# Batch 0 of clustered attention with a token mixer: mixed tokens turned by VectorE in 32x32 blocks, stored and gathered by DMAs, in place of transposes on TensorE

## The chip, the cores and the metric

One core of a Trainium2 chip runs the kernel. The metric is the device time of one execution in microseconds (us), lower is better. The runs of one kernel agree to within about 0.2%.

## The reference

Everything is in float32. Attention over B = 4 batches, H = 8 heads, S = 768 tokens, D = 64, where a query sees only the keys of its own cluster of 16; its output x then goes through a mixer over the tokens and one over the channels:

```python
q_assign = argmax(q_n . c_n)             # cosine, 16 centroids for each head
k_assign = argmax(k_n . c_n)
scores = where(q_assign == k_assign, q @ k.T / 8, -1e9)
x = softmax(scores) @ v                  # heads side by side: (4, 768, 512)
u = x + ((x.T @ U) @ V).T                # U 768x32, V 32x768: tokens mixed
out = u + relu(u @ w_ch1) @ w_ch2        # 512 -> 2048 -> 512
```

## The kernel before

**Attention** goes by 16 pairs of heads, four for each batch (`NP = 4`); a pair's heads i lie in 128 partitions. For each pair the tokens are assigned to clusters (`sims`, `clusters`), the row maxima are found from products on TensorE that VectorE reduces (`rowmax`: matmuls in line 2174, reductions in 2176), the scores are made transposed and go through the exponential on ScalarE (`scores`, 2202 and 2204), the sums are collected on GpSimd and VectorE (`weights`, 2232), the products with V are made (`values`, 2240), and the result is turned back and divided by the sums into `xt`, tokens in partitions (`normalise`, 2273 and 2274). The products of `rowmax`, `clusters`, `mix_v` and others share four PSUM banks (pool `ps_w`, `work(name)`).

**The mixer over tokens** follows at the end of each batch. `mix_u` and `mix_sum` make x^T U. For batch 0 `mix_v` (matmul in 2324, addition on VectorE in 2325) adds the product with V to `xt` itself, so that `xt` holds u; `store_u` writes it to the DRAM tensor `u_scr`. For batches 1 to 3 `turn_x` (2285) turns each pair's part of `xt` in blocks of 32x32 on VectorE, in halves h of 384 tokens, and `store_x` (2290) writes that to the DRAM tensor `x_blk`; later `fetch_columns` (2542) gathers it from there with the channels in partitions, in pieces of 128 bytes.

**The channel mixer** needs u with channels in partitions, in a high and a low part of FP32R type. For batch 0 it runs as a plain product, in two halves i of 384 tokens: `fetch_u` loads 384x512 of u from `u_scr` into the buffer "R" (2357); `turn_u(i, d)` makes, for each of four blocks d of 128 channels, three transposes on TensorE into a PSUM bank (2363), a copy on ScalarE to the high part (2365) and a subtraction on VectorE to the low part (2366); `gemm1` (2374 to 2376), `after_gemm1` (2383), `gemm2` (2393 to 2395) and `finish` follow for 16 blocks of the hidden width. `finish` adds the rows that `fetch_u` loaded. Batches 1 to 3 run by seven products of half-sized blocks (`seven1`, `seven2`).

**The order** is written out by hand. The planner collects events `at(time, function, arguments)`; the times come from the tables `times`, `mixes` and `stages`, and the table `shifts` moves single events. They are sorted by time, each function issues its instructions, and `keep_order` (line 1827) keeps every engine in just that order. The unit of time is one step of the attention's loop; `M0` is the start of batch 0's `gemm1`. SyncE (SP) issues the DMAs, in the same order. The lines that set the events of the steps here:

```python
if i >= NP:
    at(when(f"normalise{h}", i) + 0.35, turn_x, i, h)
    at(when(f"normalise{h}", i) + 0.9, store_x, i, h)
...
at(m + (-11.79 if i else -15.06), fetch_u, i)
for d in range(ND):
    at(m + (-4.5 + d if i else -7 + 0.6 * d), turn_u, i, d)
```

Which of a pool's buffers a tile gets is left to the pool, by turns.

The engines in the views: PE is TensorE's matmuls, PEld its weight loads, DVE VectorE, ACT ScalarE, POOL GpSimd. "Busy" of PE counts pipelined records, which overlap.

## Time and profile before

| what | value |
|---|---|
| time, median of 3 runs | 909.28 us |
| lowest and highest of the runs | 909.24 and 911.18 us |
| profiled execution, first to last instruction | 908.0 us |
| PE busy in the whole span | 893.4 us |
| DVE, ACT, POOL busy in the whole span | 734.8, 451.0, 614.7 us |
| granted TensorE clock, mean | 1.000 |

The profile shows one execution. Its span is the time from its first to its last instruction; the device time of the runs also counts what lies around that, 1.28 us by the median. A time of its own is not given for the profiled execution, so the span stands beside the runs' median. A busy engine is not yet the one that sets the time: the chain that ended last tells on whom the end waits, and the list of waits of an engine when it stood still and for whom.

### The profile page before, as it was taken

Reading aid. Unit: us, or ns where it says so; the run is one execution under the profiler, and the core shown is the slowest. Engines: PE = TensorE matmul, PEld = TensorE weight load, DVE = VectorE, ACT = ScalarE, POOL = GpSimd, SP = SyncE. Lnnn points to the kernel's source line nnn. Section 1 sums busy time; section 2 is a strip of 40 time slices with the busy share of each in tenths; the row PEclk is TensorE's granted clock in tenths of the full one; section 3 lists DMA queues with packets and bytes.
Section 4 is the critical chain, followed back from the end, with each engine's and each line's share of the span. In section 5 each row is a group of like instructions: output and inputs, shape, how many; then the busy total and the mean of one; then the engine's idle time right before and its main releaser. Section 6 shows DMA issues by size and latency. Waiting matters only on the chain.

```text
span 908.0 us, 15012 instructions
## 1 busy us (share of the span) xinstructions
PE 893.4 (98%) x5157; PEld 762.2 (84%) x5157; DVE 734.8 (81%) x1387; ACT 451.0 (50%) x801; POOL 614.7 (68%) x472
## 2 busy tenths in 40 slices
PE   5999999999999999999999999999999999999998
PEld 2767767777677777768898999999999999999998
DVE  7999989999999997798885366767889778897777
ACT  6646555555555556674755444533334424363330
POOL 3678759998879999962748856733578424875337
PEclk9999999999999999999999999999999999999999
DMA  8765845777486763678998996998676997769653
GB/s 228 182 155 139 205 119 145 225 196 183 127 203 162 200 174 83 184 240 265 287 305 283 294 366 240 322 308 276 222 286 214 354 248 295 258 241 327 233 194 116
DMA packets 123068, 206.25 MB, mean 227 GB/s; under 512 B 46545, under 2 KB 90385, under 8 KB 118513
## 3 DMA queue, kind: packets, MB, share of 16 engines
q1 hardware_dynamic: 122464, 205.10, 73.4%
q8 instruction: 41, 0.67, 0.3%
q10 hardware_dynamic: 528, 0.20, 0.1%
q14 instruction: 35, 0.28, 0.1%
HBM read 131.96 MB, written 42.83 MB: 193 GB/s over the span
## 4 chain that ended last, share of the span: by engine, by line
PE 95%; ACT 2%; DMA 1%; DVE 0%; SPq 0%; POOL 0%; issue 0%; ACTq 0%; DVEq 0%
PE st L2202 14%; PE o_ps L2240 14%; PE ps_max L2174 7%; PE ps_q L2684 4%; PE ps_q L2686 4%; PE ps_q L2685 4%; PE ps_p L2609 4%; PE ps_p L2608 4%; PE ps_p L2610 4%; PE ps_p L2686 3%; PE ps_p L2684 3%; PE ps_p L2685 3%; PE ps_q L2608 3%; PE ps_q L2609 3%; PE ps_q L2610 3%; PE ps_h L2374 3%
## 5 line engine op out<-in xcount | busy, mean ns | idle before, releaser
L2176 DVE TENSOR_REDUCE m<-ps_max 128x1 f32<-128x384 f32 x384 | 189.8, 548 | 17.4 <-PE ps_max L2174 15.0
L2232 POOL TENSOR_TENSOR T<-T,pr 128x768 f32<-128x768 f32 x95 | 178.7, 1885 | 21.9 <-DVE T L2232 13.3
L2204 ACT ACTIVATE pr<-st 128x768 f32<-128x768 f32 x192 | 154.6, 812 | 69.0 <-PE st L2202 58.1
L2202 PE MATMUL st<-arena 128*128 128x384 f32 (+1 forms) x768 | 169.4, 344 | 0.0
L2202 PEld LDWEIGHTS st<-arena 128*128 128x128 f32 (+1 forms) x768 | 137.3, 190 | 4.3 <-issue 1.8
L2240 PE MATMUL o_ps<-pr,vt 128*64 128x384 f32 x768 | 129.8, 490 | 0.0
L2240 PEld LDWEIGHTS o_ps<-pr,vt 128*64 128x64 f32 x768 | 52.8, 137 | 66.8 <-issue 62.4
L2174 PE MATMUL ps_max<-arena 128*128 128x384 f32 x384 | 106.3, 358 | 2.2 <-DVE arena L2139 1.5
L2174 PEld LDWEIGHTS ps_max<-arena 128*128 128x128 f32 x384 | 70.8, 194 | 14.6 <-DVE m L2176 4.9
L2608 PE MATMUL ps_p<-arena,w 128*128 128x384 f32 x186 | 62.2, 334 | 0.0
L2610 PE MATMUL ps_p<-arena,w 128*128 128x384 f32 x186 | 62.2, 334 | 0.0
L2609 PE MATMUL ps_p<-arena,w 128*128 128x384 f32 x186 | 62.2, 334 | 0.0
L2232 POOL TENSOR_TENSOR T<-pr 128x768 f32<-128x768 f32 x23 | 43.6, 1896 | 18.9 <-ACT pr L2204 18.8
L2608 PE MATMUL ps_q<-arena,w 128*128 128x384 f32 x150 | 50.2, 334 | 0.0
L2610 PE MATMUL ps_q<-arena,w 128*128 128x384 f32 x150 | 50.2, 334 | 0.0
L2609 PE MATMUL ps_q<-arena,w 128*128 128x384 f32 x150 | 50.1, 334 | 0.0
L2244 ACT COPY os<-o_ps 128x384 f32<-128x384 f32 x32 | 15.2, 480 | 65.3 <-PE o_ps L2240 62.0
L2101 POOL TENSOR_TENSOR arena<-R,arena 128x768 fp32r<-128x768 f32 x17 | 31.8, 1870 | 22.2 <-ACT arena L2096 22.1
L2232 POOL TENSOR_TENSOR Tv<-Tv,pr 128x768 f32<-128x768 f32 x21 | 40.3, 1921 | 4.1 <-DVE Tv L2232 3.0
L2670 POOL TENSOR_TENSOR h<-ring,h 128x384 fp32r<-128x384 f32 x17 | 17.6, 1032 | 37.6 <-ACT h L2660 18.6
L2609 PEld LDWEIGHTS ps_p<-arena,w 128*128 128x128 f32 x186 | 34.9, 188 | 0.1
L2608 PEld LDWEIGHTS ps_p<-arena,w 128*128 128x128 f32 x186 | 34.9, 188 | 0.1
(588 smaller groups left out, 2354.1 us busy)
## 6 DMA issues: line engine op xcount, KB each, us to landing
w<-wc SPq DMA_DIRECT2D x24, 1024.0 KB
w<-wc SPq DMA_DIRECT2D x25, 768.0 KB
arena<-wc SPq DMA_DIRECT2D x19, 768.0 KB
rw<-in_w SPq DMA_DIRECT2D x27, 512.0 KB
R<-in_qk SPq DMA_DIRECT2D x32, 384.0 KB
arena<-arena SPq DMA_DIRECT2D x31, 384.0 KB
arena<-arena SPq DMA_DIRECT2D x62, 192.0 KB
wc<-f SPq DMA_DIRECT2D x46, 256.0 KB
```

What stands on the lines that cost most here:

```text
L2174: nc.tensor.matmul(ps[:, 0:HS], x1[:, 0, g // 2, g % 2, t * P:(t + 1) * P], x1[:, 1, h, g % 2, :], start=True, stop=True)
L2176: nc.vector.reduce_max(live["m2", i][:, h, u:u + 1], ps[:, 0:HS], axis=AX.X)
L2202: nc.tensor.matmul(st[:, k, 0:HS], keys, x[0:rows_, 0, h, j, :], start=not last, stop=last)
L2204: nc.scalar.activation(pr, st[:, :, 0:HS], AF.Exp, scale=SCALE)
L2232: eng.tensor_add(T, live["p", i, h, 0] if c == 1 else T, live["p", i, h, c])
L2240: nc.tensor.matmul(o_ps[64 * j:64 * j + 64, 0:HS], vv[:, c, j, :], chunk(i, h, c, j), start=(c == 0), stop=(c == NT - 1))
L2608: nc.tensor.matmul(ps, w[:, 0, k], u[:, 0, k], start=(k == 0), stop=False)
L2609: nc.tensor.matmul(ps, w[:, 0, k], u[:, 1, k], start=False, stop=False)
L2610: nc.tensor.matmul(ps, w[:, 1, k], u[:, 0, k], start=False, stop=(k == 1))
L2684: nc.tensor.matmul(ps, w[:, 0], h[:, 0], start=(j == 0), stop=False)
L2685: nc.tensor.matmul(ps, w[:, 0], h[:, 1], start=False, stop=False)
L2686: nc.tensor.matmul(ps, w[:, 1], h[:, 0], start=False, stop=(j == 1))
```

## The change

- `x_blk[0]` becomes a DRAM tensor as for the other batches. Batch 0's four pairs go through `turn_x` and `store_x` too, behind `mix_v`, so that what is stored is u in blocks of 32x32: eight block transposes on VectorE and eight stores.
- A new `fetch_turned(h, d)` gathers these, four DMAs for each h and d (32 in all), each 32 partitions of 12 pieces of 32 elements, into a buffer `uT` of tag "R", channels in partitions.
- `turn_u` no longer uses TensorE or PSUM: the copy to the high part and the subtraction read `uT`.
- `fetch_u` moves to M0 and M0 + 9; the second half's `turn_u` moves ahead.
- A table `slots` with a class `Placed` hands out the buffers of several pools in a written order.
- Some 500 events of the plan move, by changed and added entries of `shifts`.

```diff
-    x_blk = [None, *(dram.tile([NT, P, DM], F32, name=f"x_blk{b}") for b in range(1, B))]
+    x_blk = [dram.tile([NT, P, DM], F32, name=f"x_blk{b}") for b in range(B)]
...
-    def turn_u(i, d):
-
-        ps = work("ps_uT")
-        for t in range(HT):
-            nc.tensor.transpose(ps[:, t * P:(t + 1) * P], live["u", i][:, t, d * P:(d + 1) * P], ident)
-        hi, lo = (x[:, d, :] for x in turned[i % 2])
-        nc.scalar.copy(hi, ps[:, 0:HS])
-        nc.vector.tensor_sub(lo, ps[:, 0:HS], hi)
+    def fetch_turned(h, d):
+
+        if ("uT", h) not in live:
+            live["uT", h] = rows.tile([P, ND, HS], F32, name="uT", tag="R")
+        x = x_blk[0].rearrange("(h t) (a r) (d k c) -> h d k r (t a) c", h=2, a=4, d=ND, k=4)[h, d]
+        y = live["uT", h][:, d].rearrange("p (n c) -> p n c", c=32)
+        for k in range(4):
+            nc.sync.dma_start(out=y[32 * k:32 * k + 32], in_=x[k])
+
+    def turn_u(h, d):
+
+        x = live["uT", h][:, d]
+        hi, lo = (x[:, d, :] for x in turned[h])
+        nc.scalar.copy(hi, x)
+        nc.vector.tensor_sub(lo, x, hi)
...
             if i >= NP:
                 at(when(f"normalise{h}", i) + 0.35, turn_x, i, h)
                 at(when(f"normalise{h}", i) + 0.9, store_x, i, h)
+            else:
+                at(NS * NP + (17.0, 13.0)[1 - h] + (1.6, 1.8)[1 - h] * i, turn_x, i, h)
+                at(NS * NP + (17.01, 13.01)[1 - h] + (1.6, 1.8)[1 - h] * i, store_x, i, h)
...
-        at(m + (-11.79 if i else -15.06), fetch_u, i)
         for d in range(ND):
-            at(m + (-4.5 + d if i else -7 + 0.6 * d), turn_u, i, d)
+            at(M0 + (-19.9 if i else -29.9) + 2 * d, fetch_turned, i, d)
+        at(M0 + (9 if i else 0), fetch_u, i)
+        for d in range(ND):
+            at(m + (-14.5 + 1.2 * d if i else -7 + 0.6 * d), turn_u, i, d)
...
+class Placed:
...
+    def tile(self, shape, dtype, name, tag=None, **kind):
+        turn = self.turns.get(tag or name)
+        if turn is not None:
+            return self.pool.tile(shape, dtype, name=name, tag=f"{tag or name}_{next(turn)}", bufs=1)
+        if tag is not None:
+            kind["tag"] = tag
+        return self.pool.tile(shape, dtype, name=name, **kind)
```

Where the rows of the instructions move, by the line numbers of each program (a line from 2050 on stands some 247 lines later in the changed one):

TensorE, in batch 3 of attention, shortly ahead of the expert layers of batch 0. Before, three and six transposes of u stand between the scores (`st`) and the products with V (`o_ps`):

```order
L2202 MATMUL st<-arena 128x384 x8
L2186 MATMUL ps_mT<-ident,m 12x128
L2363 MATMUL ps_uT<-ident,u 128x128 x3
L2240 MATMUL o_ps<-pr,vt 64x384 x10
L2260 MATMUL ps_sumT<-ident,sums 128x128 x3
L2273 MATMUL ps_oT<-ident,os 128x128 x3
L2202 MATMUL st<-arena 128x384 x8
L2363 MATMUL ps_uT<-ident,u 128x128 x6
L2202 MATMUL st<-arena 128x384 x8
L2240 MATMUL o_ps<-pr,vt 64x384 x14
```

The same place in the changed program:

```order
L2433 MATMUL ps_mT<-ident,m 12x128
L2499 MATMUL ps_sum<-T,sel 32x384 x2
L2499 MATMUL ps_sum<-Tv,sel 32x384 x2
L2487 MATMUL o_ps<-pr,vt 64x384 x10
L2507 MATMUL ps_sumT<-ident,sums 128x128 x3
L2520 MATMUL ps_oT<-ident,os 128x128 x3
L2449 MATMUL st<-arena 128x384 x8
L2487 MATMUL o_ps<-pr,vt 64x384 x14
L2449 MATMUL st<-arena 128x384 x8
```

The transposes are gone, the sums of a pair (`ps_sum`) come earlier, and the products with V stand ahead of the next scores.

VectorE, in batch 1 of attention, where the additions of `mix_v` (`xt<-ps_h,xt`) stand among the reductions of the row maxima (`m<-ps_max`). Before:

```order
L2325 TENSOR_TENSOR xt<-ps_h,xt 128x512
L2176 TENSOR_REDUCE m_1634<-ps_max 128x1 x4
L2325 TENSOR_TENSOR xt<-ps_h,xt 128x512
L2176 TENSOR_REDUCE m_1634<-ps_max 128x1 x2
L2325 TENSOR_TENSOR xt<-ps_h,xt 128x512
L2176 TENSOR_REDUCE m_1634<-ps_max 128x1 x8
L2176 TENSOR_REDUCE m_1937<-ps_max 128x1
```

The changed program from the same addition on:

```order
L2572 TENSOR_TENSOR xt<-ps_h,xt 128x512
L2423 TENSOR_REDUCE m_1635<-ps_max 128x1 x2
L2532 STREAM_TRANSPOSE xs_1844<-xt 128x384
L2423 TENSOR_REDUCE m_1635<-ps_max 128x1 x3
L2572 TENSOR_TENSOR xt<-ps_h,xt 128x512 x2
L2423 TENSOR_REDUCE m_1635<-ps_max 128x1 x5
L2532 STREAM_TRANSPOSE xs_1924<-xt 128x384
L2572 TENSOR_TENSOR xt<-ps_h,xt 128x512
L2423 TENSOR_REDUCE m_1635<-ps_max 128x1
L2532 STREAM_TRANSPOSE xs_1941<-xt 128x384
```

The first three block transposes (`xs`) stand there now, between the reductions; the other five follow with one to five reductions or some work of the clusters between them.

SyncE, some way ahead of the expert layers. Before:

```order
L2318 DMA x_scr_93<-x_2993 96x512
L1875 DMA rw<-in_w 128x512
L2056 DMA vt<-in_v 128x768
L1875 DMA rw<-in_w 128x512
L2357 DMA u<-u_scr 128x1536
```

And in the changed program, where the gathers (`uT`) stand:

```order
L2197 DMA arena<-ones 1x12x128 x2
L2613 DMA uT<-x_blk_90 32x12x32 x4
L2122 DMA rw<-in_w 128x512 x2
L2673 DMA wc_0_99<-w_98 256x1x256 x2
L2613 DMA uT<-x_blk_90 32x12x32 x4
L2537 DMA x_blk_92<-xs_4406 128x3x128
L2613 DMA uT<-x_blk_90 32x12x32 x12
```

The load of u is gone from here (it is issued later); 20 of the 32 gathers stand among loads of weights (`rw`).

## Rows read from the trace of the kernel before

**Rows 1.** The page: span, and the chain that ended last by engine.

```profile
span 908.0 us, 15012 instructions
...
PE 95%; ACT 2%; DMA 1%; DVE 0%; SPq 0%; POOL 0%; issue 0%; ACTq 0%; DVEq 0%
```

**Rows 2.** PE's waits, the longest: waiting line, releaser, us in total, times, longest.

```profile
PE ps_c L1994 <- ACT rw_g L1992: 7.5, 2, 5.1
```

**Rows 3.** Stretch, its us; busy us of PE, PEld, DVE, ACT, POOL; clock, DMA, GB/s.

```profile
65.00:900.00 835.00, 835.00 (x4876) 724.03 (x4877) 673.49 (x1255) 412.80 (x731) 576.81 (x410) 1.00 0.74 231
150.00:195.00 45.00, 45.00 (x280) 33.90 (x278) 41.36 (x81) 27.55 (x39) 42.38 (x25) 1.00 0.66 199
336.00:390.00 54.00, 54.00 (x344) 39.15 (x342) 42.09 (x84) 32.32 (x51) 52.24 (x30) 1.00 0.52 141
440.00:480.00 40.00, 40.00 (x211) 36.48 (x210) 32.64 (x53) 25.45 (x50) 19.72 (x16) 1.00 0.88 282
```

**Rows 4.** Tile of the transposes: duration in ns min/median/max, first and last start.

```profile
L2363 PE MATMUL ps_uT<-ident,u x24: 270/272/328, 380.5 to 471.4; 128*128 128x128 f32 x24
...
L2366 DVE TENSOR_TENSOR arena<-ps_uT,arena x4: 519/532/551, 383.8 to 404.9; 128x384 fp32r<-128x384 f32 x4
```

**Rows 5.** PE's timeline in the expert layers: start, us, instruction.

```profile
466.46 0.39 PE L2395 MATMUL y<-arena,hx 128*128 128x512 f32 x1
466.69 0.49 PE L2363 MATMUL ps_uT<-ident,u 128*128 128x128 f32 x3
466.93 0.42 PE L2374 MATMUL ps_h<-arena,w1h 128*128 128x384 f32 x1
467.19 0.34 PE L2375 MATMUL ps_h<-arena,w1h 128*128 128x384 f32 x1
467.36 0.34 PE L2376 MATMUL ps_h<-arena,w1l 128*128 128x384 f32 x1
```

**Rows 6.** PE's timeline in attention, each group of transposes with what follows.

```profile
380.48 0.49 PE L2363 MATMUL ps_uT<-ident,u 128*128 128x128 f32 x3
380.90 3.45 PE L2240 MATMUL o_ps<-pr,vt 128*64 128x384 f32 x20
...
386.40 0.82 PE L2363 MATMUL ps_uT<-ident,u 128*128 128x128 f32 x6
386.97 1.67 PE L2202 MATMUL st<-arena 128*128 128x384 f32 x8
...
401.38 0.55 PE L2363 MATMUL ps_uT<-ident,u 128*128 128x128 f32 x3
401.68 0.59 PE L2202 MATMUL st<-arena 128*128 128x384 f32 x2
```

**Rows 7.** DVE: the block transposes by line, and the page's group of row maxima.

```profile
L2285 DVE STREAM_TRANSPOSE xs<-xt x24: 520/569/579, 190.0 to 447.1; 128x384 f32<-128x384 f32 x24
...
L2176 DVE TENSOR_REDUCE m<-ps_max 128x1 f32<-128x384 f32 x384 | 189.8, 548 | 17.4 <-PE ps_max L2174 15.0
```

**Rows 8.** Gathers of batches 1 to 3: SP's issue, and DMA of 500 to 524 us.

```profile
L2542 SPq DMA_DIRECT2D f<-x_blk x48: 309/525/3347, 500.3 to 744.1; - x48
...
DMA packets 17212, 6.79 MB, mean 283 GB/s; under 512 B 12158, under 2 KB 17111, under 8 KB 17209
...
f<-x_blk SPq DMA_DIRECT2D x16, 96.0 KB
```

**Rows 9.** Timelines of DVE and POOL: an operation with two inputs in SBUF.

```profile
388.94 1.82 DVE L1924 TENSOR_TENSOR arena<-rw_t,arena 128x512 fp32r<-128x512 f32 x1
393.20 0.68 DVE L1924 TENSOR_TENSOR arena<-rw_t,arena 128x512 fp32r<-128x512 f32 x1
...
384.54 7.91 POOL L2232 TENSOR_TENSOR T<-T,pr 128x768 f32<-128x768 f32 x4
```

**Rows 10.** DVE's timeline at the first expert block; the matmuls that need it.

```profile
414.93 1.02 DVE L2383 SCALAR_TENSOR_TENSOR hx<-ps_h,hx 128x384 fp32r<-128x384 f32 x2
...
L2393 PE MATMUL y<-w,hx x24: 387/390/500, 419.3 to 500.1; 128*128 128x512 f32 x24
```

748 lines of the change are left out of this document (490 added, 258 removed).

## The prediction

> **What bounds the kernel now.** I read the page's chain that ended last first: 95% of it is TensorE (PE), everything else is 2% or less [rows 1]. Then PE's own list of waits: the longest entry is 7.5 us, for the centroids at the program's start [rows 2]; what follows it in the list is smaller still. Then the busy time by stretches: from 65 to 900 us PE is busy in 835.00 of 835.00 us, at a granted clock of 1.00 [rows 3], which is the upper of its two levels (2.4 GHz). So in the whole part that the change touches PE never stands still, and two things follow: a microsecond of PE work that is taken out shortens the run by a microsecond, and any other engine costs something only from the moment when PE waits for it. VectorE (DVE), GpSimd (POOL) and the DMA engines are all less than full over that stretch [rows 3], so the question for each is local: is it late in one place.
>
> **The sum, step by step.** It is made against the profile's span of 908.0 us [rows 1]. The median of the three runs, 909.28, stands 1.28 us above that span, for what lies around it, and I add the same 1.28 at the end.
>
> *1. PE loses 24 transposes.* The trace records 272 ns for each [rows 4], which would be 24 x 0.272 = 6.5 us. But PE works pipelined, and its records overlap, so I go by starts. They stand in eight groups of three, and each group can be priced by when the work behind it starts. In the expert stage, a matmul that stands in front of another starts 0.23 us before the next thing, the group of three takes 0.24 us from its start to the next start, and the first matmul behind it takes 0.26 us to the second, where matmuls without a neighbour of another kind are 0.17 us apart [rows 5]. So a group costs 0.24 + 0.09 = 0.33 us. The other three groups of that stage, at 445, 460 and 471 us, show 0.25 each. In the attention stage the same reading gives 0.42, 0.57 (for two groups that stand together) and 0.30 us [rows 6]. The sum: 0.42 + 0.57 + 0.30 + 4 x 0.245 = 2.27 us from start to start, plus 0.09 behind each of six of the seven places, less 0.09 for the first group, in front of which a transpose stood and behind which the work changes kind anyway. This is **2.7 us** that PE gains. Lower bound: 24 x 0.08 = 1.9 us, when only the 0.24 us of the cheapest group [rows 5] counts for each of eight. Upper bound: the 6.5 us of the recorded durations.
> The Trainium skill, page "TensorE: Matmul & The Clock Gate", Part 4 (PE-mode transpose), gives a 128x128 transpose about 275 ns in one kernel's context; for 24 in full that is an estimate of 6.6 us. The recorded duration agrees (272 ns [rows 4]), but the starts do not: PE goes on after a third of it [rows 5].
>
> *2. The order of attention's work on PE changes as well*, at many places. No instruction but the transposes goes or comes there. What a new order can cost PE by itself is a change from one kind of matmul to another, 0.09 us each [rows 5]; leaving out the transposes, the changed program has some three such changes more, under 0.3 us. I take nothing, with 0.3 us either way.
>
> *3. DVE gains eight block transposes of batch 0*, at 569 ns, the median of the 24 that it already makes for the other batches [rows 7]: 8 x 0.569 = 4.55 us. By the order they stand among the row maxima and the adds of the mixer, at about 158 to 190 us. There DVE is busy in 41.36 of 45.00 us [rows 3], so 3.64 us are free and at least 0.91 us are not covered. The change also moves other DVE work around this place, and PE does not feel a late row maximum at once, since four PSUM banks lie between the two engines, and DVE's reduction of one takes 548 ns [rows 7]: 4 x 0.548, some 2 us. I take nothing, by that cover; if it is gone, between 0.9 and all 4.55 us reach PE.
>
> *4. SyncE (SP) issues eight more stores and 32 gathers.* At the 525 ns that a gather takes it for the other batches [rows 8], 40 x 0.525 = 21 us of SP, in pieces spread over 200 us. SP's share of the chain is 0% [rows 1]. The loads of weights that are queued behind the gathers come up to 16.8 us (32 of them) later, and PE's list of waits holds none for a weight. Taken as nothing; a late weight would show as a PE wait.
>
> *5. The DMA engines carry 32 gathers* of 49 KB in 128-byte pieces, 12,288 pieces. The same number (16 gathers of 96 KB) goes through in 24 us at 500 to 524 us, when the engines are busy all the time and also carry weights [rows 8]; so the pieces cost at most 24 us of DMA time. Where they are gathered, at 336 to 390 us, the engines are busy for a share of 0.52 of the 54 us [rows 3], so 26 us are free. Nothing on PE. On the other hand, the two plain loads of u (768 KB each) move into a fuller place, 0.88 busy at 440 to 480 us [rows 3], but they now have to be there only for the last addition.
>
> *6. The splitting of u into high and low parts* reads SBUF and no longer PSUM. ScalarE's four copies a half change their source alone. DVE's subtraction (0.53 us [rows 4]) now has two inputs in SBUF. An operation of that kind took 1.82 us while POOL was in the middle of four long additions, and 0.68 us once they had ended [rows 9]. So each of the first half's four subtractions, near 385 to 392 us, may grow by the same factor of 2.7, to 1.4 us: 4 x 0.9 = 3.5 us more of DVE at worst, none at best. At the end of this, DVE's first work for the expert layers ends at 415.95 us, and PE wants it at 419.3 [rows 10]: 3.35 us ahead, some 2 us once PE runs earlier by the four groups in front of it (0.42 + 0.57 + 0.30, and 0.1). The value I take is the inner one, 0: a delay of up to 2 us is hidden; beyond that up to 1.5 us come through.
> The Trainium skill, page "SBUF — State Buffer", section "SBUF: two separate sides", says that DVE with two SBUF inputs and POOL lock each other out of a shared port for the length of an instruction. It speaks against this part of the change; the trace agrees, with 1.82 against 0.68 us [rows 9].
>
> Sum: -2.7 + 0 + 0 + 0 + 0 + 0 = -2.7 us. The span would be 905.3 and the time **906.6 us**.
>
> **The rivals.** 0.2% of the time (1.8 us) is about what a measurement of this kernel can tell from no change; faster means below 907.46, slower above 911.1.
>
> *Given back at the block transposes.* DVE's 0.91 uncovered us at 158 to 190 reach PE, and up to two thirds of the rest of the 4.55: 907.5 to 909.9 us. For it: 41.36 of 45.00 us [rows 3]. Against it: the four banks, and PE does not stand still anywhere behind 65 us so far [rows 3].
>
> *Given back at the subtractions.* POOL's additions hold the first half's four subtractions at 1.4 us each, and 1.5 us come through to the first expert layers: 906.6 + 1.5 = 908.1 us, with the half of it 907.5 at the least. For it: the long row of [rows 9]. Against it: the 2 us of slack, and that POOL's additions end at 392.45 us [rows 9], while the last of the four subtractions so far starts at 404.9 [rows 4]. The lock that the Trainium skill's page "SBUF — State Buffer" states is what this rival would be.
>
> *DVE's block transposes all reach PE* (the other side). The reductions queued behind each block transpose on DVE hold PSUM banks; the block transposes of one half share one staging buffer, so that each also waits until the store before it has landed, and PE's row-maximum matmuls stand still once four banks are full. The price is 8 x 0.569 = 4.55 us and the landings: -2.7 + 4.55 = +1.85, that is 911.1 us and above, up to 913 with 0.3 us of landing for each of six. It decides from the point where DVE falls behind by more than the 2 us of the four banks in more than two or three places. For it: DVE has its narrowest place just there [rows 3]. Against it: eight are spread over 30 us, and the order puts one to five reductions between two of them.
>
> *More than forecast.* The transposes hold PE for their recorded 272 ns after all: 909.28 - 6.5 = 902.8 us. The Trainium skill's figure (Part 4, above) would be this case. Against it stand the starts [rows 5, 6]; the truth can lie in between, or the new order saves its 0.3 us too.
>
> *The change does not do what it says.* The order of instructions shows the 24 transposes gone, so this I give nothing.
>
> **How the numbers follow.** Forecast, 905.4 to 907.46: 0.60. Given back at the block transposes, 907.46 to 909.9: 0.12; at the subtractions, to 908.1, or both together, to 911.1: 0.10. All of DVE's transposes: 0.12. More than forecast, 902.8 to 905.4: 0.06. So faster is 0.60 + 0.06 = 0.66, same 0.22, slower 0.12. The time is the forecast's, 906.6. The range goes down to 905.4 (PE's 2.7 us, with 0.3 of new order and almost 1 more out of the upper bound) and up to 910.9, which takes in everything that is given back in part; outside are the rival of all the transposes and the bigger gain, 0.18.
>
> **What would show it.** Right: no PE row for the transposes; PE still busy for all of 65 to 900 us; the expert layers and the last matmul some 2.7 us earlier, and half of that already before the first expert layer. Wrong in part 3: PE's waits name the reductions of the row maxima at 158 to 195 us, and the work behind is later, not earlier. Wrong in part 6: subtractions of 1 us and more, and PE waiting for them or for DVE's expert work at 405 to 420 us. Wrong in part 5: a PE wait for a weight or for the gathered tokens at 380 to 550 us. Wrong in part 1: PE full everywhere, and the time shorter by 5 us or more.

## The result, and the profile after

The changed kernel takes 919.75 us (median of 4 runs, 917.47 to 920.02), the kernel before beside it 909.78 us (909.24 to 911.18): a ratio of 1.0101, 95% interval 1.0087 to 1.0115. It is slower by 1%, some 10 us, where 2.7 us of gain were forecast; the time lies outside the range. The runs of one version scatter more than the 0.2% given above: by up to 4 us, and the kernel before too (909.06 to 912.73 us in fifteen runs), so a difference of a microsecond between two versions says little. The profiled execution took 919.68 us with a span of 917.9 us.

The page of the changed kernel: span, busy time by engine, and the chain that ended last by engine.

```profile
span 917.9 us, 14997 instructions
PE 896.3 (98%) x5133; PEld 760.9 (83%) x5133; DVE 745.0 (81%) x1395; ACT 451.2 (49%) x801; POOL 614.3 (67%) x472
PE 80%; DVE 9%; ACT 4%; DMA 3%; issue 2%; POOL 1%; SPq 0%; DVEq 0%; ACTq 0%
```

The chain was 95% PE before [rows 1]; now it is 80%, with 9% over DVE and 3% over DMA. PE's waits in the changed kernel between 65 and 900 us, where before there was none (waiting line, releaser, us in total, times, longest):

```profile
PE st L2449 <- ACT pr L2451: 3.2, 1, 3.2
PE ps_xu L2545 <- DVE hx L2637: 2.0, 1, 2.0
PE ps_max L2421 <- DMA arena<-arena: 0.8, 1, 0.8
PE ps_max L2421 <- DVE rw_t L2143: 0.5, 1, 0.5
PE y L2647 <- ACT hx L2636: 0.4, 1, 0.4
PE ps_max L2421 <- DVE oh L2332: 0.2, 1, 0.2
```

The windows of [rows 3] again, in the changed kernel (same columns), and behind them 4 us from just behind the first long wait, the 4 us that follow, and 4 us around the second long wait:

```profile
65.00:900.00 835.00, 827.64 (x4796) 712.06 (x4789) 675.85 (x1249) 412.72 (x731) 566.02 (x401) 1.00 0.76 233
150.00:195.00 45.00, 43.47 (x264) 31.84 (x262) 42.97 (x86) 26.19 (x38) 38.33 (x22) 1.00 0.75 205
336.00:390.00 54.00, 53.91 (x339) 37.32 (x337) 43.64 (x84) 30.54 (x47) 51.79 (x30) 1.00 0.57 135
440.00:480.00 40.00, 38.42 (x193) 32.82 (x194) 31.18 (x50) 25.50 (x50) 22.73 (x18) 0.96 0.90 289
...
397.00:401.00 4.00, 3.84 (x14) 3.75 (x15) 3.30 (x6) 3.89 (x8) 0.00 (x0) 0.57 1.03 284
401.00:405.00 4.00, 4.00 (x30) 3.08 (x28) 3.93 (x6) 3.48 (x6) 1.29 (x1) 1.00 0.83 256
...
441.00:445.00 4.00, 3.42 (x18) 1.20 (x19) 3.71 (x8) 4.00 (x9) 3.93 (x4) 0.57 0.82 278
```

Two things are to be seen. PE, full before, stands still for 835.00 - 827.64 = 7.36 us. And right behind each of the two long waits the granted clock is 0.57: PE runs most of those 4 us at the lower level (1.2 GHz), and is back at 1.00 in the 4 us that follow the first of them. So these two waits cost more than their rows say.

Where the 9.9 us of span (917.9 - 908.0) come from can be read by pairing the same matmuls in both traces and subtracting their starts. Times in this table are those of the kernel before.

| place | lag added, us | what the changed trace shows there |
|---|---|---|
| 121 to 175 us, and 0.5 up to 369 | 3.1 | waits of 0.5 (DVE), 0.8 (DMA), 0.2 (DVE); the rest are delays too short to show as idle time |
| 387 to 394 us | 4.6 | the wait of 3.24, then the lower clock: 1.2 to 1.4 |
| 428 to 445 us | 4.0 | the wait of 1.95, then the lower clock: about 1.7 |
| 484 us | 0.8 | `y` waits for ACT's `hx` |
| the eight groups of transposes gone | -2.6 | drops of 0.39, 0.47 (two groups), 0.38, 0.32, 0.42, 0.29; the eighth, under the rise at 445, taken at their mean, 0.32 |

That is 12.5 - 2.6 = 9.9 us. (The lags are counted from zero. The changed trace starts 0.3 us ahead, before 120 us, where PE's order is still the same; against that start the places add up to 0.3 us more.) The long waits can be followed back on the timeline of the changed kernel (start, us, engine, line, operation, count; in brackets the idle time before it and what ended it):

```profile
382.13 13.40 POOL L2479 TENSOR_TENSOR T<-T,pr 128x768 f32<-128x768 f32 x7
...
388.01 2.64 SPq L2613 DMA_DIRECT2D uT<-x_blk  x4
390.75 0.41 SPq L2122 DMA_DIRECT2D rw<-in_w  x1
...
389.88 4.00 DVE L2620 TENSOR_TENSOR arena<-uT,arena 128x384 fp32r<-128x384 f32 x2 [0.92 <-DMA vt<-in_v]
...
396.43 0.56 DVE L2620 TENSOR_TENSOR arena<-uT,arena 128x384 fp32r<-128x384 f32 x1 [0.34 <-ACT arena L2619]
...
395.33 0.67 ACT L2130 ACTIVATE rw_g<-rw 128x512 f32<-128x512 f32 x1 [4.55 <-DMA rw<-in_w]
395.90 0.50 ACT L2619 CAST arena<-uT 128x384 fp32r<-128x384 f32 x1
396.30 0.81 ACT L2451 ACTIVATE pr<-st 128x768 f32<-128x768 f32 x1
...
397.16 2.92 PE L2449 MATMUL st<-arena 128*128 128x384 f32 x8 [3.24 <-ACT pr L2451]
...
404.94 1.65 PE L2449 MATMUL st<-arena 128*128 128x384 f32 x8
...
441.58 1.93 PE L2545 MATMUL ps_xu<-xt,u_w 128*32 128x512 f32 x8 [1.95 <-DVE hx L2637]
```

At 397.16 PE waits for an exponential (`pr`) of ACT. ACT was not slow: it stood for 4.55 us on a weight (`rw`), whose load SP had issued at 390.75, behind four gathers that took SP 2.64 us. In a run without the turns, stores and gathers (below) the same weight is issued at 384.47, and PE has no such wait. So PE's list names ACT, and the trace shows the cause in a queue two steps back. The eight score matmuls behind the wait take 2.92 us, the same eight at 404.94 take 1.65: that is the clock. On DVE, two subtractions of u take 4.00 us beside POOL's seven additions, and 0.56 us each once these have ended. At 441.58 the order has the product `ps_xu` of batch 3's mixer ahead of an expert block, on a PSUM bank that DVE's `hx` frees only then.

### The profile page after: what moved, and what is told of

Its sections match the earlier page's. It is cut to its first block, busy times and chain, and to the rows that moved or that the text cites. A ratio compares the mean times of both kernels' runs of the same rounds, so it can differ in the third digit from the quotient of the medians.

```text
span 917.9 us, 14997 instructions
## 1 busy us (share of the span) xinstructions
PE 896.3 (98%) x5133; PEld 760.9 (83%) x5133; DVE 745.0 (81%) x1395; ACT 451.2 (49%) x801; POOL 614.3 (67%) x472
## 4 chain that ended last, share of the span: by engine, by line
PE 80%; DVE 9%; ACT 4%; DMA 3%; issue 2%; POOL 1%; SPq 0%; DVEq 0%; ACTq 0%
PE st L2449 13%; PE o_ps L2487 10%; PE ps_max L2421 7%; PE ps_q L2940 4%; PE ps_q L2938 4%; PE ps_q L2939 4%; PE ps_p L2862 4%; PE ps_p L2863 4%; PE ps_p L2864 4%; PE ps_p L2940 3%; PE ps_p L2938 3%; PE ps_p L2939 3%; PE ps_q L2862 3%; PE ps_q L2864 3%; PE ps_q L2863 3%
## 5 line engine op out<-in xcount | busy, mean ns | idle before, releaser
L2421 PE MATMUL ps_max<-arena 128*128 128x384 f32 x384 | 108.6, 361 | 3.7 <-DVE arena L2386 1.5
```

Source lines behind the costliest of these rows:

```text
L2421: nc.tensor.matmul(ps[:, 0:HS], x1[:, 0, g // 2, g % 2, t * P:(t + 1) * P], x1[:, 1, h, g % 2, :], start=True, stop=True)
```

## The experiments

Each was timed against the kernel before on the same chip; its medians there lay between 909.5 and 910.9 us. Theory at this point: the 10 us are lateness on DVE and on SP's queue at three places, and mending these gives the forecast back. Rival: the order is so full that a wait taken away at one place comes back at the next.

### On the changed kernel: mend one wait, take one part away

**Gathers of the second half's third channel block earlier on SP**, so that the weight at 390.75 isn't queued behind them.

```diff
+    "fetch_turned 1 2": -6.24,
```

> One row of the plan moves in the changed kernel: the four gathers of the second half's block d = 2, which stand directly ahead of a load of weights on SyncE, are issued with the twelve before them, some 12 us earlier. Theory (SyncE's queue delays that load by the 2.64 us of the four gathers, ScalarE's copy of the loaded weights waits for it with the exponential queued behind, and TensorE stands still for 3.24 us): the load lands 2.6 us earlier, TensorE's wait for the exponential shrinks from 3.24 to about 0.6 us, the 1.2 us at the lower clock behind it go, and the time falls by 2.6 to 4 us, to 916 to 917 us. Rival (VectorE's subtractions with two SBUF inputs, 4.0 us for two, hold the scores up): the wait stays, 919 to 920 us.

Measured: 919.5 us, 1.0106 (1.0089 to 1.0123). PE's 3.2 us for ACT are gone, and 2.6 us for DVE's `rv` stand at the same place. This new wait is the edit's own making, as the timelines of SP and DVE show:

```profile
372.85 13.96 SPq L2614 DMA_DIRECT2D uT<-x_blk  x16
...
390.06 0.58 DVE L2533 STREAM_TRANSPOSE xs<-xt 128x384 f32<-128x384 f32 x1 [4.47 <-DMA x_blk<-xs]
```

The four gathers now stand in a row of sixteen that holds SP for 13.96 us. A store of `xs` is queued behind them, and DVE stands 4.47 us for its staging buffer, ahead of `rv`; the slow subtractions come only behind `rv` in DVE's order. The weight itself is issued at 390.39, hardly earlier than 390.75. So this run doesn't test the mend that it was meant to test.

**Subtractions later**, out from under POOL's additions.

```diff
-    "turn_u 0 3": -9.01719087,
+    "turn_u 0 3": -6.75,
-    "turn_u 0 2": -7.89770833,
+    "turn_u 0 2": -6.14,
```

> In the changed kernel the first half's copies and subtractions of blocks d = 3 and 2, the two that took 4.0 us beside GpSimd's 13.4 us of additions, move behind those of d = 1 and 0, to where GpSimd is idle. Theory (the shared port makes each of them 2 us instead of 0.55): two subtractions of 0.55 us, VectorE some 2.9 us freer; TensorE's wait at 393 us stays, since it hangs on a load of weights, and the second wait, at 441 us for the expert work on VectorE, shrinks if VectorE's delay came from here: 916 to 919.7 us. Rival (that second wait comes from the order of VectorE's work around it): no change outside 0.5 us, 919.2 to 920.

Measured: 920.82 us, 1.0117 (1.0099 to 1.0134). PE's wait for `pr` is 3.7 us: it is still set by the weight, for which ACT stands 5.8 us, and the two subtractions, now 0.56 and 0.55 us, win nothing here.

**Six of the eight block transposes left out.**

```diff
+        if 0 < i < NP:
+            return
```

> In the changed kernel only pair 0 of batch 0 is turned in blocks (two of the eight block transposes); the stores of pairs 1 to 3 store pair 0's blocks again, so all eight stores and all gathers stay, and the output of batch 0 is left wrong. Theory (TensorE's 2.8 us of delay between 140 and 178 us come from VectorE's 4.55 us of block transposes): with 3.4 us of them gone the delay falls by 1.5 to 2.8 us, 917 to 918.3 us. Rival A (it comes from SyncE, where the stores and the wait for them stand ahead of the DMAs that place the keys): delay stays above 2 us, 919 to 920. Rival B (the new order of the attention's events alone): the same as rival A in time, but with the waits for VectorE still there.

Measured: 921.83 us, 1.0129 (1.0108 to 1.0149). Between 140 and 190 us the lag grows by 1.6 instead of 2.9 us, so the six block transposes hold about half of what is lost there; the total is no better (919.6 to 923.55), and the two later waits stay (3.1 and 2.0 us).

**Two plain loads in place of the 32 gathers.**

```diff
-        for k in range(4):
-            nc.sync.dma_start(out=y[32 * k:32 * k + 32], in_=x[k])
+        if d == 3:
+            nc.sync.dma_start(out=live["uT", h].rearrange("p d n -> p (d n)").rearrange("p (t m) -> p t m", t=HT),
+                              in_=u_scr[:, h * HT:(h + 1) * HT, :])
```

> In the changed kernel the 32 gathers are replaced by two plain loads of the same 768 KB each from the rows of u, issued where the fourth block's gathers stood; what the expert layers of batch 0 then compute on is not turned, so the output of batch 0 is left wrong. Theory (the gathers cost by SyncE's time, not by the block transposes): as in the run with the four gathers moved, the wait at 393 us falls to about 0.6 us and the time by 2.6 to 4 us, and not much more, since the other 28 gathers stand where nothing waits on SyncE: 915.5 to 917 us. Rival (all 32 gathers hurt, by their 128-byte pieces in the DMA engines): 913 to 915 us.

Measured: 918.71 us, 1.0097 (1.0071 to 1.0122). The wait for `pr` is gone; 1.4 and 0.7 us for DVE's weights (`rw_t`) are left there, the 2.0 us of `ps_xu` stay, and PE waits 2.1 us for a load of keys at 165 us. The four runs lie apart, two at 916.7 and 917.0 and two at 920.5 and 921.0 us, and the profile is of the slowest. Without any gather the kernel is still 7 to 11 us slower, so the gathers aren't the bulk of it.

**Bank of `ps_xu`**: two digits of the written order of PSUM banks exchanged.

```diff
-        "...203203120123102130213203203012103210..."
+        "...203203120123102130213203201032103210..."
```

> In the changed kernel two digits of the written order of PSUM banks change places: the mixer's product of batch 3 takes bank 1, which the expert block 5 has left by then, and the expert block 7 takes bank 3, which the mixer had and which block 3 leaves only at 441.5 us. Theory (TensorE's second wait, 1.95 us at 441 us, hangs on that choice of bank, and the 1.7 us at the lower clock behind it on that wait): both go, 3.6 us less, 916 us. Rival (VectorE is late at that place whatever the bank): TensorE waits for VectorE's next expert work instead, a microsecond later, and the time falls by less than 1.5 us.

Measured: 921.32 us, 1.0117 (1.01 to 1.0134). The wait of `ps_xu` is gone; `ps_rep`, the next step of the same mixer, waits 1.4 us for ACT instead.

**The three mends together** (gathers earlier, subtractions later, bank).

```diff
+    "fetch_turned 1 2": -6.24,
...
+    "turn_u 0 3": -6.75,
...
+    "turn_u 0 2": -6.14,
...
+        "...203203120123102130213203201032103210..."
```

> The changed kernel with three edits at once: the four gathers issued earlier, the two subtractions behind GpSimd's additions, and the two digits of the order of banks. Theory (at 393 us two late paths stand side by side, the load behind the gathers and VectorE behind the subtractions, so that each edit alone only showed the other): neither wait is left, nor the lower clock behind them; 919.75 less 3.2 + 1.2 + 2.0 + 1.7 = 8.1 us, 911.7 us, and up to 914 if a smaller wait takes their place. Rival (the order of attention is late by itself): 916 us and more.

Measured: 920.38 us, 1.0104 (1.0089 to 1.0119). Nothing is won. The row of sixteen gathers is here too and holds SP for 13.75 us, a store of `xs` is queued behind it, DVE's next block transpose waits 4.46 us for the staging buffer, and PE 2.6 us for DVE. At the second place PE waits 1.7 us for `ps_rep`, as with the bank alone.

On the changed kernel none of the mends is faster by what its wait was long. At the second place (bank) the rival holds: the wait comes back at the next step. At the first it isn't decided, since the two runs that move the gathers make the new wait themselves. What was not tried is a place for the gathers where nothing is queued behind them; the run without any gather bounds what that could give, to 1 us by the medians and 3 us by its two faster runs.

### The order and the work apart

**The new order with the old work**: transposes back on PE, no block transposes, stores or gathers.

```diff
-        x = live["uT", h][:, d]
+        k = next(b for b, y in used if not any(y is z for z in live.values()))
+        ps = ps_w.pool.tile([P, 512], F32, name="ps_uT", tag=f"w_{k}", bufs=1)
...
+        for t in range(HT):
+            nc.tensor.transpose(ps[:, t * P:(t + 1) * P], u[:, t, d * P:(d + 1) * P], ident)
```

> The changed kernel's order of events and its written order of buffers, with the work of the kernel before: batch 0's u is turned by TensorE from plainly loaded rows (24 transposes, a PSUM bank each time that no other tile holds), without the eight block transposes, the eight stores and the 32 gathers. Theory A (the new work causes the loss; the order alone is worth about nothing): 909 to 911 us, no wait of TensorE at 393 us. Theory B (the new order and the written buffers are late by themselves): 914 us and more, with the wait at 441 us (2 us, and 1.7 us of lower clock behind it) still there.

Measured: 923.22 us, 1.0136 (1.0121 to 1.0151). This run can't be read as the order alone: the transposes need a PSUM bank that the new order hasn't got, and PE waits 3.4, 2.2 and 1.7 us around them.

**The new work in the old order.**

```diff
-            at(M0 + (-19.9 if i else -29.9) + 2 * d, fetch_turned, i, d)
+            plan.append((GATHER[i][d], len(plan), fetch_turned, (i, d)))
...
-                at(NS * NP + (17.0, 13.0)[1 - h] + (1.6, 1.8)[1 - h] * i, turn_x, i, h)
+                plan.append((TURN[h][i], len(plan), turn_x, (i, h)))
...
```

> The other way round: the kernel before with its own order and its pools' own choice of buffers, and the new way of turning batch 0's u put in: the eight block transposes and stores behind the additions of the mixer, the 32 gathers where the last loads of queries and keys are done, no transposes on TensorE. Theory A (the new work causes the loss): 914 us and more, with TensorE's waits for VectorE at 158 to 180 us and for the subtractions or the loads at 385 to 400 us. Theory B (the order does): 906.6 to 910 us, 2.5 us of transposes gained and up to 2.8 us lost beside the block transposes.

Measured: 926.75 us, 1.0173 (1.0158 to 1.0188), with waits of 3.0 (a load of V), 2.7, 2.6 (in two) and 1.8 us (all for DVE); the lag is 11 us by 185 us already. Why it is so dear shows in two waits, of DVE and of SP, between 145 and 195 us (waiting line, releaser, us, times, longest):

```profile
DVE xs L2285 <- DMA x_blk<-xs: 5.2, 4, 2.3
SPq L2290 <- DVE xs L2285: 15.3, 7, 4.7
```

DVE's block transposes stand 5.2 us until a store has freed their staging buffer, and SP stands 15.3 us for block transposes whose stores are next in its order, with the loads of V and of keys behind. In the same stretch of the changed kernel DVE has no such wait, and SP one of 8.8 us. With the new order the same work is 10.0 us slower than the kernel before (919.75 - 909.78): the order mends 5.9 of the 15.9 us (926.75 - 910.89) that the work costs in the old one.

**The new order without the new work and without PE's transposes**: two plain loads, no turns, no stores, subtractions from SBUF; the written order of buffers stays.

```diff
-            else:
+            elif False:
                 at(NS * NP + (17.0, 13.0)[1 - h] + (1.6, 1.8)[1 - h] * i, turn_x, i, h)
                 at(NS * NP + (17.01, 13.01)[1 - h] + (1.6, 1.8)[1 - h] * i, store_x, i, h)
...
-        for k in range(4):
-            nc.sync.dma_start(out=y[32 * k:32 * k + 32], in_=x[k])
+        if d == 3:
+            nc.sync.dma_start(out=live["uT", h].rearrange("p d n -> p (d n)").rearrange("p (t m) -> p t m", t=HT),
+                              in_=u_scr[:, h * HT:(h + 1) * HT, :])
```

> The changed kernel's order and buffers with as little of the new work as can be: no transposes on TensorE, no block transposes, no stores of batch 0, two plain loads of u's rows in place of the 32 gathers; the copies and the subtractions with two inputs in SBUF stay. What the expert layers of batch 0 compute on is not turned, so its output is left wrong. By the prices measured one at a time on the order of before (gathers 5 to 6.6 us, block transposes 2.7, stores 2.7, subtractions 2.2) and TensorE's gain of 2.6: if the order is worth nothing by itself, 909.3 - 2.6 + 2.2 = 909 us. Rival (the new order is late by itself, 1.5 us at 140 to 178 us and 3.7 us at 441 us): 913 to 915 us.

Measured: 917.11 us, 1.0074 (1.0057 to 1.0091). PE's longest waits between 65 and 900 us in this run (two of 0.5 and 0.4 us are left out), and the first of them on PE's timeline:

```profile
PE ps_xu L2545 <- DVE hx L2636: 1.9, 1, 1.9
PE ps_sum L2499 <- DVE rw_t L2143: 1.4, 1, 1.4
PE y L2646 <- ACT hx L2635: 0.9, 2, 0.5
PE ps_oT L2520 <- DVE rw_t L2143: 0.7, 1, 0.7
...
438.52 1.07 PE L2545 MATMUL ps_xu<-xt,u_w 128*32 128x512 f32 x8 [1.95 <-DVE hx L2636]
```

This is the run that settles most. It is 6.9 us slower than the kernel before (917.11 - 910.22; the lag of its matmuls ends at 6.9 too), with the transposes' 2.6 us saved: it loses 9.5 of the changed kernel's 12.5 us with none of the turns, stores and gathers in it. Of the 9.5, 2.5 are lost between 387 and 400 us, around the subtractions; the other 7.0 go with the new order and the written order of PSUM banks that belongs to it, which no run parts. What the turns, stores and gathers still cost in the new order is 12.5 - 9.5 = 3.0 us. This split is good to some 0.8 us: this trace starts 0.5 us late, the changed one 0.3 early. Paired matmul by matmul from 140 us on, the changed kernel loses 3.9 us more than this run, 1.3 of them between 150 and 180 us and 2.1 between 380 and 410. The costs of order and work also don't simply add: the order costs some 7 us without the work, and with it saves 6.

**The expert block put ahead of `ps_xu` again**, in that run and in the changed kernel.

```diff
-    "gemm1 0 7": -0.5458333325,
+    "gemm1 0 7": -2.5679,
...
-        "...203203120123102130213203203012103210..."
+        "...203203120123102130213203210302103210..."
```

> The kernel of the run before in this list, with the twelve matmuls of expert block 7 put ahead of batch 3's mixer product again, as in the kernel before, with the banks that this order needs. Theory (the wait at 441 us comes from that one exchange in the order): 2 us of wait and 1.7 us at the lower clock go, 3 to 4 us less than that run. Rival (VectorE's chain of weight loads is late there in any order): within 1 us of it.

> The whole changed kernel with that one exchange undone (block 7 of the experts ahead of batch 3's mixer product). Theory: 919.75 less 2 to 3.7 us, 916 to 918 us. Rival (the delay from 393 us on is passed down VectorE's chain and is met here in any order): 919 to 920 us.

Measured: 916.89 us, 1.0074 (1.0059 to 1.0089), against 917.11 without the exchange; and 921.67 us, 1.0122 (1.0103 to 1.0141). The wait of `ps_xu` is gone in both, and this row has taken its place (the first of PE's waits in the first of the two):

```profile
PE y L2646 <- ACT hx L2635: 2.0, 2, 1.6
```

This fits the rival: the exchange moves the wait 40 us on. That the work of ACT and DVE is late as a whole is the likely reading, not a shown one.

### One part alone, on the kernel before

**The gathers alone**: 32 gathers of batch 1's stored blocks into u's buffer, in rows of up to twelve, ahead of the plain load as it was.

```diff
+    GATHER = ((155.4980, 156.5, 157.5, 158.5), (166.92, 168.5, 169.5, 170.6))
...
+        for d in range(ND):
+            plan.append((GATHER[i][d], len(plan), fetch_turned, (i, d)))
```

> The kernel before, whose TensorE waits for nothing between 65 and 900 us, with one part of the new work added and nothing else: the 32 gathers (they read batch 1's blocks, which lie there by then, into the buffer that the plain load of u fills afterwards, so what is computed stays). They stand where they stood in the run with the new work on the order of before. Theory (their 17 to 25 us of SyncE's time hold the loads of weights, of V and the stores behind them up): TensorE waits 2 to 5 us in all between 360 and 410 us, 911.5 to 916 us. Rival (they fall into free time of SyncE and the DMA engines): 909 to 910.5 us.

Measured: 916.46 us, 1.0085 (1.0067 to 1.0102). Its timeline on SP and PE:

```profile
373.23 11.38 SPq L2365 DMA_DIRECT2D u<-x_blk  x12
384.65 1.26 SPq L2427 DMA_DIRECT2D wc<-w  x2
386.01 0.56 SPq L2290 DMA_DIRECT2D x_blk<-xs  x1
...
390.04 1.83 PE L2371 MATMUL ps_uT<-ident,u 128*128 128x128 f32 x6 [3.28 <-DVE rv L2262]
```

and the row of its waits between 340 and 420 us that joins the two:

```profile
DVE xs L2285 <- DMA x_blk<-xs: 5.5, 1, 5.5
```

Twelve gathers in a row hold SP for 11.38 us. Batch 3's store is queued behind them; DVE stands 5.5 us until that store has landed and its staging buffer is free; PE stands 3.28 us for DVE.

**The same 32 gathers, spread**: sixteen in a stretch in which SP has nothing else, the rest in fours.

```diff
-    GATHER = ((155.4980, 156.5, 157.5, 158.5), (166.92, 168.5, 169.5, 170.6))
+    GATHER = ((155.4980, 156.5, 156.51, 156.52), (156.53, 157.5, 166.92, 169.5))
```

> The kernel before with the 32 gathers alone, as in the run with the gathers alone, but placed where SyncE has nothing to issue: 16 of them in the 11 us at 352 to 363 us in which it waited for a buffer, the rest in three fours. Theory (what the gathers cost is what waits behind them in SyncE's queue, there a store of 192 KB whose one staging buffer VectorE needs): VectorE's wait of 5.5 us for that store and TensorE's of 3.3 us go, 909.5 to 912 us. Rival (the 12,288 pieces of 128 bytes load the DMA engines, wherever they stand): 914 to 917 us.

Measured: 910.51 us, 1.0003 (0.9993 to 1.0014). On SP, with what follows:

```profile
349.12 8.69 SPq L2365 DMA_DIRECT2D u<-x_blk  x16
362.91 0.36 SPq L1875 DMA_DIRECT2D rw<-in_w  x1
```

and the window of [rows 3] over the long stretch:

```profile
65.00:900.00 835.00, 834.75 (x4873) 723.95 (x4870) 668.17 (x1254) 412.26 (x730) 576.85 (x410) 1.00 0.75 232
```

PE is full again but for 0.25 us. The same gathers, the same 12,288 pieces of 128 bytes, cost 6.6 us or nothing; what differs is where they stand on SP, and the chain of waits above goes over what is queued behind them. The Trainium skill, page "DMA: Bandwidth & Descriptors", section "Specifications", gives 512 bytes as the smallest transfer that goes at full rate. No run here measures the rate of these pieces; in this one no cost of them reaches the time.

**Subtractions with two inputs in SBUF, nothing else.**

```diff
-        nc.vector.tensor_sub(lo, ps[:, 0:HS], hi)
+        nc.vector.tensor_sub(lo, live["u", i].rearrange("p t m -> p (t m)")[:, d * HS:(d + 1) * HS], hi)
```

> The kernel before with one change: the eight subtractions of the expert layers' low parts read their first input from the loaded rows in SBUF and no longer from PSUM (of the wrong elements, so the output of batch 0 is left wrong; shape, place and number stay). Theory (VectorE and GpSimd share a port when VectorE has two SBUF inputs): the two or three of them that fall beside GpSimd's 7.9 us of additions take up to 2 us instead of 0.53, VectorE comes 3 to 4 us later at 385 to 393 us and 1 to 3 us of it reach TensorE: 910.5 to 913 us. Rival (it stays hidden): 909 to 910 us.

Measured: 912.03 us, 1.0023 (1.0014 to 1.0033). The row of the first half's tile (min/median/max in ns), where [rows 4] had 519/532/551, and the longest one with what POOL did beside it, from the timeline:

```profile
L2366 DVE TENSOR_TENSOR arena<-u,arena x4: 1016/1314/2168, 383.9 to 406.9; 128x384 fp32r<-128x384 f32 x4
```

```profile
391.31 2.17 DVE L2366 TENSOR_TENSOR arena<-u,arena 128x384 fp32r<-128x384 f32 x1
...
384.64 8.41 POOL L2232 TENSOR_TENSOR T<-T,pr 128x768 f32<-128x768 f32 x4
```

The first half's subtractions cost 2.2 us of time, through PE waits of 0.35, 0.27 and 0.76 us and shorter delays; the second half's wait for nothing that PE needs. The Trainium skill, page "SBUF — State Buffer", section "SBUF: two separate sides", says that the one of DVE and POOL that loses the shared port is blocked outright. The rows agree: 2.17 us beside POOL's additions, 0.56 us in the changed kernel when POOL has ended.

**The eight block transposes alone; the eight stores alone** (straight from batch 0's tokens).

```diff
+    TURN = ((60.8345, 62.7430, 64.44085, 68.3), (64.4940, 64.5380, 70.0, 71.51205))
...
+            else:
+                t = TURN[h][i]
+                plan.append((t, len(plan), turn_x, (i, h)))
```

> The kernel before with the eight block transposes of batch 0 added on VectorE at the places of the run with the new work on the order of before, without the stores; nothing reads what they write. Theory (VectorE's 4.55 us at its narrowest place reach TensorE, in part): 2 to 4.5 us, 911.5 to 914.5 us, by waits for the row maxima at 160 to 180 us. Rival A (covered by the PSUM banks): 909 to 910.5 us. Rival B (more than the transposes' own time, since TensorE loses its clock or a chain of VectorE's work starts later): 915 us and more.

> The kernel before with the eight stores of batch 0 added at the same places, taken straight from the attention's result without the block transposes; nothing reads what they store. Theory (the block transposes are the cost, the stores only queue on SyncE): 909 to 911 us. Rival (SyncE and the DMA engines are what is late at 160 to 180 us, by the DMAs that place keys behind the stores): 912 to 918 us, with TensorE waiting for a DMA.

Measured: block transposes 912.53 us, 1.0031 (1.0019 to 1.0043); stores 912.61 us, 1.0039 (1.0024 to 1.0054). From the timeline with the block transposes:

```profile
168.06 0.28 PE L2186 MATMUL ps_mT<-ident,m 128*12 128x128 f32 x1 [1.08 <-DVE m L2181]
```

and with the stores:

```profile
160.47 5.06 SPq L2291 DMA_DIRECT2D x_blk<-xt  x3
...
168.80 0.43 SPq L2056 DMA_DIRECT2D vt<-in_v  x1
169.23 3.12 PE L2240 MATMUL o_ps<-pr,vt 128*64 128x384 f32 x18 [2.32 <-DMA vt<-in_v]
```

With the block transposes PE loses 2.9 us between 145 and 178 us; 1.08 us of that show as one wait, the rest as delays too short to show. The stores put a load of V, issued at 160.66 us by the kernel before, 8.1 us back on SP, and PE waits 2.32 us for it.

Together, from the medians: gathers 6.6, subtractions 2.2, block transposes 2.7, stores 2.7, less 2.6 for PE's transposes: some +11.5 us. All of it at once in the old order measured +15.9, so at these places the parts also make each other dearer; the two waits between block transposes and stores that are shown there need both.

### A version that the single parts point to

By these runs the gathers are free in SP's free stretch, and the second half's subtractions cost nothing where they stood. So only the second half of batch 0 was moved off PE, in the old order.

```diff
+    def turn_mixed(p):
+        x = live["xm", p] = (sb if p % 2 else late).tile([P, HS], F32, name=f"xm{p}", bufs=1, tag=("xs", "sims")[p % 2])
+        nc.vector.transpose(x.rearrange("p (t d) -> p t d", t=HT), live["x", 0][:, HT:NT, p * P:(p + 1) * P])
...
+    TURN, STORE, GATHER = (69.6, 71.51205, 71.51685, 71.575), (69.61, 71.51206, 71.6005, 71.6006), (156.5, 156.51, 156.52, 156.53)
```

> The kernel before, its order kept, with the change applied to the second half of batch 0 alone: four block transposes, four stores, sixteen gathers issued in SyncE's free stretch around 350 us, and the half's twelve TensorE transposes gone; the first half stays on TensorE. Theory (what the change costs is what waits for the steps it adds and moves, and the single parts add up): the twelve transposes gone give 1.36 us (half of 2.7), the gathers cost nothing at that place (as in the run with gathers spread), the second half's subtractions cost nothing (as in the run with two SBUF inputs), and what is left is the four block transposes and the four stores: half of 2.7 and 2.7 us at most, nothing at best, so 908.5 to 910.5 us against 909.9 for the kernel before. Rival (any work added to VectorE or SyncE ahead of 180 us is paid in full): over 911.5 us.

A second version also puts DVE's join of one expert block's weights 12 steps later:

```diff
+    OV = {'load_weights 0 2 2': 83.4899}
```

> The kernel of the run before with one more edit: VectorE's join of expert weights for expert block 2 is put 12 steps later in the order, out of the stretch in which the block transposes are added. Theory: if the block transposes cost by lateness on VectorE between 70 and 180 us, the 2.1 us that the join takes there are given back to the waits, and the time is 0.3 to 1 us under the run before; rival (the cost is at SyncE's stores, or there is none): within 0.3 us of the run before.

Measured: 917.07 us, 1.0073 (1.0059 to 1.0086), and 916.87 us, 1.0072 (1.006 to 1.0085) with the join later. Both expectations of the theory fell. By 200 us the first of them has lost 6.3 us; from there to 440 us, past all gathers, it loses no more, and the twelve transposes give back 1.3 us, as expected. But behind 470 us it loses 1.1 us again: the second half's subtractions take up to 1.67 us here, and PE waits 0.8 us for the last one, so that they aren't free either. Its timeline, and SP's wait in the same stretch:

```profile
185.43 1.15 SPq L2293 DMA_DIRECT2D x_blk<-xm  x2
186.62 1.20 SPq L1950 DMA_DIRECT2D arena<-arena  x2
...
177.29 0.54 DVE L2290 STREAM_TRANSPOSE xm<-xt 128x384 f32<-128x384 f32 x1
...
189.35 0.59 PE L2174 MATMUL ps_max<-arena 128*128 128x384 f32 x2 [2.53 <-DMA arena<-arena]
...
SPq L2293 <- DVE xm L2290: 9.0, 2, 6.6
```

and the granted clock right behind that wait, with, under it, the same behind the wait of 2.32 us in the run with the stores alone:

```profile
189.00:193.00 4.00, 3.65 (x13) 3.68 (x14) 2.04 (x4) 0.81 (x1) 3.84 (x3) 0.62 0.92 296
```

```profile
169.00:173.00 4.00, 3.77 (x24) 2.12 (x26) 3.88 (x7) 1.69 (x3) 4.00 (x3) 1.00 1.05 338
```

Four block transposes and four stores cost 6.3 us here, more than the 2.7 and 2.7 of eight of each alone. They stand later: the last block transpose starts at 177.29, against 171.13 with the eight alone, and the last stores go out at 185.43, against 167.88. SP stands 9.0 us for the block transposes whose stores it has to issue next. The load of V that it issued at 160.66 in the kernel before goes out at 170.77, and the keys' load of 178.72 at 186.62, just behind two of the new stores; the lower clock (0.62) adds its part to PE's 2.53 us. How the 6.3 us divide among these isn't settled. With the join later, PE waits 1.4 us for DVE instead of the 2.53 for the load and loses 1 us less by 200 us, but 1.8 us more at 420 to 430 us, where the join now stands. No version tried here beats the kernel before.

## Why the prediction was wrong

**Step 1, the transposes, was right.** 2.7 us were forecast from the starts, the changed trace shows 2.3 in seven of the eight groups, 2.6 with the eighth. Neither the recorded 272 ns nor the rival that took them at full length holds.

**Step 2, the order, failed, and by most.** It priced PE's list alone: three changes of kind, 0.3 us. A new order on PE is also a new set of due times for the engines that feed it. The run with the order and without turns, stores and gathers loses 9.5 us, some 7.0 of them from the order and its written banks. PE's own sequence doesn't show it; the place to look is DVE's and ACT's work ahead of each moved matmul (the bank that `hx` frees for `ps_xu`, the weights that `rw_t` makes for `ps_sum`), though no reading of that kind was tried ahead of a run. Which of the some 500 moves, or of the banks, cost what isn't settled: the two exchanges that were tried only moved the wait.

**Step 3, the block transposes**, was taken as nothing, by the cover of four banks. Alone they cost 2.7 us, between the two bounds given (0.9 and 4.55). The cover isn't there in [rows 3]: DVE had 3.64 us free in 45, and its lateness also reaches PE by other ways than the row maxima, by `mT` of the same pair, and by SP, which stood 8.8 us for block transposes between 145 and 195 us in the changed kernel, with loads behind. The rival on the other side (all block transposes reach PE) had the sign and the place, not the size. Its mechanism, a block transpose that waits until the store before it has landed, is what the new work in the old order shows: 5.2 us in four waits of DVE, where 0.3 us for each was taken without a row.

**Step 4, SP**, failed in its reason: that SP has no share of the chain says that nothing waited for it before, not that it may be late. Eight stores cost 2.7 us, most of it through one load of V, 32 gathers 6.6 us in rows of up to twelve and nothing in a free stretch. The gather's 0.525 us [rows 8] isn't always the price either: the changed kernel's row of twelve took SP 6.47 us (0.54 each), the row of twelve in the old order 11.38 (0.95 each).

**Step 5, the pieces on the DMA engines**, was right: nothing.

**Step 6, the subtractions**, had the mechanism and not the size. 1.4 us at worst was estimated for each, 2.0 were measured for two of them in the changed kernel and up to 2.17 alone; 2.2 us came through, where 0 was taken and 1.5 was the upper end. The additions of POOL were read to end at 392.45 [rows 9], so that the last of the four subtractions would stand free at 404.9. But the same trace has POOL at the next addition from 404.42 to 406.25 us, and the fourth subtraction took 1.43 us there when it had two inputs in SBUF; in the changed kernel the long row ends at 395.53.

**The sum and the range.** Each rival on the slow side gave back one part. Steps 2, 3, 4 and 6 failed together and in the same direction, since they all lean on one thought: PE never stands still, so its feeders have slack. And the price of a wait was taken as its length, without what the clock takes behind it, 1.2 to 1.7 us at two places. The range ended at 910.9; the sum of the upper bounds that the text itself names (4.55, 1.5, 0.3) is already 913.

## What to carry to other kernels

An engine that is full without a wait tells nothing of how late its feeders may be: before adding work to them, look for each added step what is queued behind it on that engine or queue, and how early that is ready now. A store that stands in the queue right behind the work it waits for holds up everything behind it. Price a DMA by the loads and stores behind it on the issuing queue, and put a row of small ones where the queue is empty. Work of 2.7 us taken off a full engine is worth nothing if the place where it goes has no measured slack, and a tuned order, once changed, has to be priced anew on every engine.

## What the runs showed of the hardware

- A PE wait is often followed by the lower clock: granted 0.57 behind waits of 3.24 and 1.95 us in the changed kernel, 0.62 behind one of 2.53. It isn't the length of the wait alone: behind 2.32 us with the stores alone the clock stayed at 1.00. The same wait of `ps_xu` at the same place, 1.95 us in both traces, was followed by 0.57 in the changed kernel, where its eight matmuls took 1.93 us, and by 1.00 with the order alone, where they took 1.07. What decides it was not settled.
- The time that SP takes to issue gathers isn't fixed: sixteen took 8.69 us (0.54 each) in SP's free stretch and twelve 6.47 us (0.54 each) in the changed kernel, but twelve took 11.38 us (0.95 each) with the gathers alone and sixteen 13.96 us (0.87 each) with four of them moved. What decides it was not settled.
- A subtraction on DVE with both inputs in SBUF took from 0.56 to 2.17 us, by what POOL did beside it; with one input in PSUM it took 0.53 [rows 4].
